# The token loop of an FFT, FFN and MoE kernel: activation by ACT's sine, copies and subtraction on VectorE

## The chip, the core and the metric

The kernel runs on one core of a Trainium2 chip. The metric is the device time of one execution in microseconds (us). A core has five engines, each with an instruction queue of its own that is worked off in order: TensorE (PE in the profile; its weight loads are PEld) multiplies matrices into PSUM; VectorE (DVE) and ScalarE (ACT) work element by element on PSUM and SBUF; GpSimd (POOL) works on SBUF; SyncE (SP) issues DMAs. Engines wait for each other by semaphores.

## What is computed

Eight sequences of 3072 tokens with 256 features go through a filter in the frequency domain, a feed-forward network and a mixture of eight experts with one expert per token.

```python
X = np.fft.rfft(x, axis=1)
y = np.fft.irfft(X * (filt_r + 1j * filt_i), n=3072, axis=1)       # 8 x 3072 x 256
x = y.reshape(24576, 256)
h = x @ w_in                                                       # 256 -> 2048
g = h * np.tanh(np.log1p(np.exp(h)))
x = g @ w_out                                                      # 2048 -> 256
e_idx = np.argmax(x @ w_gate, axis=1)                              # one expert of 8 per token
for e in range(8):
    m = e_idx == e
    ye = np.maximum(x[m] @ w1[e], 0) @ w2[e]
    out[m] = softmax(x[m] @ w_gate)[e] * sigmoid(x[m] @ w_output_gate)[e] * ye
```

The factor tanh(log(1 + e^h)) is (1 - w^2)/(1 + w^2) with w = sigmoid(-h) = (1 - tanh(h/2))/2. Written as an angle it is cos(2 arctan w).

## The kernel before, in words

There are three stages. The opening (to about 150 us) prepares the weights and runs the first sequence's transform (`forward(0)`, `back(0, 0)`). The token loop (to about 2725 us) does the feed-forward network. The expert stage (to the end) runs the experts on tokens that were sorted into `bucket`.

The token loop works on tiles of 256 tokens: 12 tiles per sequence (`NT`), 96 in all. A tile has 8 units (`FP`), each with 256 of the 2048 hidden features, so there are 768 units. One step of the loop handles several units at different depths. `mm1(i)` (L821) makes `h` of unit i, 128x512 in PSUM, by 12 matmuls of fp16 high and low halves; `ps_h` has three banks for it. Then ACT takes `tanh` (L834), `arctan` (L837), `square` (L840) and `factor_c` (L844), and VectorE multiplies `h` by the three factors of a polynomial in `factor_1` (L849), `factor_2` (L853) and `product` (L857), which all read the bank. ACT writes the fp16 high half `gh` (`high_half`, L861), GpSimd the low half `gl` (`low_half`, L865). `mm2(i)` (L878) multiplies both with `w_out` by 12 matmuls into two accumulators per tile, of which there is one set. `LA` = 5: in step p, `mm1` runs for unit p + 5 and `mm2` for unit p. After the last unit of a tile, `evacuate` (L888) has ACT copy both accumulators out.

Beside this runs other work, spread over the steps by generators. `forward(b + 1)` transforms the next sequence: `psa` (L273), a round trip through DRAM (`xs`, `bin`), `psb` (L305), products on VectorE with GpSimd's sum (L311 to L325), `psbi` (L338), `zo` and a second round trip (`zs`, `zin`). `back(b, c)` brings 384 tokens back (`psai` L384, `y_h` on ACT, `y_l` on VectorE) into a ring `y_h`, `y_l`. `weights()` finds scales and writes the experts' weights as fp16 halves (L646, L678, L682). `route(g)` picks the expert of two tiles' tokens by some 20 small VectorE operations, prepares `rows` on GpSimd and ACT, and scatters them into `bucket` by indirect DMAs (L801). `units(p)` starts and advances these generators, `small()` and `big()` give the routing its turns.

The order of the instructions on each engine is written out by hand (`manual_schedule`): it is the order in which the program emits them. `post(engine, work)` puts an operation into a list, and `turn({"A": 1})` emits the next posted one of that kind (A for ACT, V for VectorE, P for GpSimd, T for TensorE, S for SyncE) if it was posted in an earlier step.

Of the kernel before, what the change touches and what calls it, by code (L numbers as in the profile page):

```python
# [22 lines left out]
D = 256  # L23
# [14 lines left out]

KAPPA = 0.2774708104398191 ** 0.5
ROOT1, ROOT2, MID, OFF = 0.17115794576, 1.30006388906, 1.33968847258, 2.69928854473  # L40
# [22 lines left out]
def fft_ffn_moe_kernel(ctx: ExitStack, tc: tile.TileContext, x, fri, w_in, w_out, w_gate, w_ogate, w1, w2,  # L63
# [196 lines left out]
    def forward(b):  # L260
# [37 lines left out]
        for g in range(NG + LAG):  # L298
            if g + 1 < NG:
                bi[g + 1] = load_bin(b, g + 1)  # L300
            if g < NG:
# [6 lines left out]
                def first(ps=ps, f=f, g=g):  # L308
                    need(g - 3)
                    yt[g] = [s1.tile([128, 2 * D], F32, tag=n, name=n, bufs=k) for n, k in (("t1", LAG + 1), ("t2", 3))]  # L310
                    nc.vector.tensor_tensor(out=yt[g][0], in0=ps, in1=f[:, 0].rearrange("p s d -> p (s d)"), op=ALU.mult)  # L311
# [295 lines left out]
    gp = ph.enter_context(tc.tile_pool(name="gp", bufs=4))  # L607
# [104 lines left out]
    def route(g, xq):  # L712
# [19 lines left out]
        r16 = rows.bitcast(F16)  # L732
        yield True
        V.tensor_reduce(out=amax, in_=xq[:, :, 0:D], axis=AX.X, op=ALU.max, apply_absolute_value=True)
        yield
        V.tensor_reduce(out=mx, in_=lg, axis=AX.X, op=ALU.max)
        yield
        V.tensor_scalar(out=amax, in0=amax, scalar1=1e-30, scalar2=None, op0=ALU.max)
        yield
        V.tensor_tensor(out=d, in0=lg, in1=col(mx), op=ALU.subtract)  # L740
# [3 lines left out]
        yield  # L744
        V.scalar_tensor_tensor(out=v, in0=d, scalar=0.0, in1=row("w8"), op0=ALU.is_equal, op1=ALU.mult)

        post("A", lambda: nc.scalar.activation(out=d, in_=d, func=AF.Tanh, scale=gates[:, 0:1]), "exp", delay=1)
# [9 lines left out]
        for s in range(RS):  # L757
# [3 lines left out]
        V.tensor_reduce(out=m2, in_=v, axis=AX.X, op=ALU.max)  # L761
        yield
        post("P", lambda: nc.gpsimd.tensor_copy(rows[:, :, D + 1:D + 2], ids_sb[:, g * RS:(g + 1) * RS].unsqueeze(2)),
             "id")
        V.tensor_tensor(out=oh[:, 0:RS, :], in0=v, in1=col(m2), op=ALU.is_equal)
        count(rank, oh)
        yield
        V.tensor_tensor(out=v, in0=oh[:, 0:RS, :], in1=lo_, op=ALU.mult)
        yield
        V.tensor_reduce(out=sel, in_=v, axis=AX.X, op=ALU.add)  # L770
        post("A", lambda: nc.scalar.activation(out=sel, in_=sel, func=AF.Sigmoid, scale=gates[:, 1:2]), "sig", delay=1)
# [17 lines left out]
        yield from until("r")  # L789
# [5 lines left out]
        yield  # L795
        V.tensor_tensor(out=rank, in0=rank, in1=oh[:, 0:RS, :], op=ALU.mult)
        yield
        with nc.allow_low_precision("whole numbers below 2^24"):
            V.tensor_reduce(out=slot, in_=rank, axis=AX.X, op=ALU.add)
# [6 lines left out]
    LA = 5  # L806
# [3 lines left out]
    h_ps, m_u, m_v, g_h, g_hl, accs = {}, {}, {}, {}, {}, {}  # L810
# [17 lines left out]
    def pair(name, bufs, dt=F32):  # L828
        return mp.tile([128, 2 * T], dt, tag=name, name=name, bufs=bufs)

    def tanh(i):
        m_u[i] = pair("u", 3)
        b = i // (FP * NT)
        nc.scalar.activation(out=m_u[i], in_=wide(h_ps[i]), func=AF.Tanh, scale=seq[b % 2][:, 1:2])  # L834

    def arctan(i):
        nc.scalar.activation(out=m_u[i], in_=m_u[i], func=AF.Arctan, scale=-0.5, bias=0.5)  # L837

    def square(i):
        nc.scalar.activation(out=m_u[i], in_=m_u[i], func=AF.Square, scale=KAPPA)  # L840

    def factor_c(i):
        m_v[i] = pair("v", 4)
        nc.scalar.activation(out=m_v[i], in_=m_u[i], func=AF.Square, bias=-MID)  # L844

    def factor_1(i):

        t = wide(h_ps[i])
        nc.vector.scalar_tensor_tensor(out=t, in0=m_u[i], scalar=-ROOT1, in1=t, op0=ALU.add, op1=ALU.mult)  # L849

    def factor_2(i):
        t = wide(h_ps[i])
        nc.vector.scalar_tensor_tensor(out=t, in0=m_u.pop(i), scalar=-ROOT2, in1=t, op0=ALU.add, op1=ALU.mult)  # L853

    def product(i):
        v = m_v[i]
        nc.vector.scalar_tensor_tensor(out=v, in0=v, scalar=OFF, in1=wide(h_ps.pop(i)), op0=ALU.add, op1=ALU.mult)  # L857

    def high_half(i):
        g_h[i] = gp.tile([128, 2 * T], F16, tag="gh", name="gh")  # L860
        nc.scalar.activation(out=g_h[i], in_=m_v[i], func=AF.Copy)  # L861

    def low_half(i):
        gl = gp.tile([128, 2 * T], F16, tag="gl", name="gl")
        nc.gpsimd.tensor_tensor(out=gl, in0=m_v.pop(i), in1=g_h[i], op=ALU.subtract)  # L865
        g_hl[i] = (g_h.pop(i), gl)

    def mm2(i):
        g, j = divmod(i, FP)
        if j == 0:  # L870
            accs[g] = [ps_acc.tile([128, NA], F32, tag=f"a{s}", name=f"a{s}") for s in range(TS)]
        gh, gl = g_hl.pop(i)
# [29 lines left out]
    gens = {"f": None, "b": back(0, 1), "r": None, "big": False}  # L902
    WE = 10
    WU, UB, BL = 390, 85, 3
# [10 lines left out]
    def units(p):  # L915
# [8 lines left out]
        if t == NT - 2:  # L924
            if j == 5 and b + 1 < NB:
                gens["b"] = back(b + 1, 0)
        elif t == NT - 1:
            if j == 3 and b + 1 < NB:
                gens["b"] = back(b + 1, 1)
        elif t % 3 and j == 1:  # L930
            gens["b"] = back(b, 2 * (t // 3) + 1 + t % 3)
# [21 lines left out]
    for p in range(-LA, nunits):  # L953

        a, c, d, e, l = p + 5, p + 4, p + 3, p + 2, p + 1
        has = [0 <= x < nunits for x in (a, c, d, e, l)]
        if has[0]:
            mm1(a)
        if p >= 1 and p % FP == 0:
            finish(p // FP - 1)  # L960
        if has[2]:
            factor_c(d)
        if has[1]:
            arctan(c)
        if has[2]:
            factor_1(d)
        if has[4]:
            low_half(l)
        if p >= 0:
            small()  # L970
            turn({"A": 1})
        if has[1]:
            square(c)
        if has[2]:
            factor_2(d)
        if p >= 0:
            small()
        if has[3]:
            high_half(e)
        if has[2]:  # L980
            product(d)
        if p >= 0:
            units(p)
            mm2(p)
            big()
            turn({"A": 1})
        else:
            piece()
        if has[0]:
            tanh(a)  # L990
        if p >= 0:
            big()
            tick()
# [298 lines left out]
```

## Time and profile before

| | us |
|---|---|
| median of 3 runs (3836.88 to 3839.9) | 3837.57 |
| the profiled execution | 3847.65 |
| its span, first to last instruction | 3845.9 |

| stage of the profiled execution | TensorE busy | ACT busy | VectorE busy | GpSimd busy |
|---|---|---|---|---|
| 200 to 2700 us, the token loop | 2417.9 | 2340.9 | 2209.2 | 1467.7 |
| 2850 to 2900 us, the expert stage | 50.0 of 50 | 16.4 | 19.5 | 8.7 |

A row of the profile names the line (L821), the engine, the operation, what it writes and reads (out<-in), shapes and types, and a count. Matmuls are pipelined: the time shown for one reaches to its modelled end, while the next has long started. The granted clock is the share of TensorE's full clock that the chip allowed in a stretch. Register, semaphore and DMA-issuing instructions are not counted as busy.

### The profile page before, as it was taken

The page shows a single profiled execution, that of the slowest core. Times are in us where ns is not written, and L with a number is a line of the kernel's source. Part 1 is how long each engine was busy: PE and PEld are TensorE (multiplying, and loading weights), DVE is VectorE, ACT ScalarE, POOL GpSimd, SP SyncE. Part 2 cuts the span into 40 slices and gives each one's busy share as a digit, 9 for nine tenths or more (in the row PEclk, how much of TensorE's full clock was granted, in tenths as well). Part 3 has the DMA queues.
Part 4 walks back from the last instruction along what each step waited for, and adds up shares of the span by engine and source line. Part 5 has one row for each costly group of instructions (what it writes and reads, how often), then busy time and mean ns, then how long its engine had stood idle before and what let it go on. Part 6 is the DMA issues. An engine that isn't in the chain of part 4 may idle for free. (4 is left out here: it accounts for less than half of the span.)

```text
span 3845.9 us, 82929 instructions
## 1 busy us (share of the span) xinstructions
PE 3652.1 (95%) x30764; PEld 3088.9 (80%) x30764; DVE 2786.5 (72%) x5395; ACT 2795.6 (73%) x5443; POOL 1757.1 (46%) x1810
## 2 busy tenths in 40 slices
PE   5699999999999999999999999999799999999998
PEld 3578887887887888787788787877588888888887
DVE  6689888988988988998898898888433333333333
ACT  3489998998998999999899999999433333333332
POOL 2346655655655665565565565555311111111111
PEclk6799999999999999999999999999899999999999
DMA  7434134223313413432432442111333434443341
GB/s 229 128 102 129 51 92 127 74 82 106 112 53 111 127 57 90 140 93 82 128 123 64 120 139 69 52 48 61 86 98 73 116 72 97 116 119 86 84 116 40
DMA packets 300743, 374.32 MB, mean 97 GB/s; under 512 B 158576, under 2 KB 242928, under 8 KB 296624
## 3 DMA queue, kind: packets, MB, share of 16 engines
q1 hardware_dynamic: 281232, 316.62, 30.3%
q0 software_dynamic: 19104, 52.39, 4.0%
q8 instruction: 241, 3.95, 0.5%
q14 instruction: 166, 1.36, 0.1%
HBM read 388.09 MB, written 121.59 MB: 133 GB/s over the span
## 5 line engine op out<-in xcount | busy, mean ns | idle before, releaser
L865 POOL TENSOR_TENSOR gl<-v,gh 128x512 f16<-128x512 f32 x768 | 891.2, 1164 | 658.0 <-ACT gh L861 617.5
L1104 DVE SCALAR_TENSOR_TENSOR hl<-eh,hh 128x256 f16<-128x256 f32 x824 | 350.0, 425 | 667.9 <-ACT hh L1103 664.1
L1103 ACT ACTIVATE hh<-eh 128x256 f16<-128x256 f32 x824 | 315.9, 383 | 667.3 <-PE eh L1094 657.9
L878 PE MATMUL a<-wout_h,gh 128*128 128x272 f16 x3072 | 751.7, 280 | 4.2 <-ACT xq L888 3.3
L878 PE MATMUL a<-wout_l,gh 128*128 128x272 f16 x3072 | 751.0, 279 | 0.0
L878 PEld LDWEIGHTS <-gh 128*128 128x128 f16 x6144 | 602.2, 98 | 178.9 <-issue 48.4
L821 PEld LDWEIGHTS <-win_h 128*128 128x128 f16 x6144 | 585.4, 98 | 182.6 <-DVE v L857 101.5
L821 PE MATMUL h<-y_h,win_h 128*128 128x256 f16 x3072 | 590.0, 274 | 65.2 <-DVE v L857 62.8
L857 DVE SCALAR_TENSOR_TENSOR v<-v,h 128x512 f32<-128x512 f32 x768 | 526.7, 686 | 168.6 <-ACT v L844 140.1
L1138 POOL DMA_INDIRECT out_dram<-ot,meta x206 | 199.7, 969 | 893.3 <-ACT hh L1103 458.0
L834 ACT ACTIVATE u<-h,seq 128x512 f32<-128x512 f32 x768 | 518.8, 676 | 111.1 <-PE h L821 110.0
L821 PE MATMUL h<-y_h,win_l 128*128 128x256 f16 x3072 | 588.1, 273 | 0.0
L821 PE MATMUL h<-y_l,win_h 128*128 128x256 f16 x3072 | 588.1, 273 | 0.0
L849 DVE SCALAR_TENSOR_TENSOR h<-u,h 128x512 f32<-128x512 f32 x768 | 527.6, 687 | 76.1 <-ACT u L840 72.2
L853 DVE SCALAR_TENSOR_TENSOR h<-u,h 128x512 f32<-128x512 f32 x768 | 531.5, 692 | 12.2
L840 ACT ACTIVATE u<-u 128x512 f32<-128x512 f32 x768 | 482.2, 628 | 16.1
L878 PE MATMUL a<-wout_h,gl 128*128 128x272 f16 x3072 | 482.9, 280 | 0.9 <-POOL gl L865 0.8
L844 ACT ACTIVATE v<-u 128x512 f32<-128x512 f32 x768 | 477.7, 622 | 0.0
L837 ACT ACTIVATE u<-u 128x512 f32<-128x512 f32 x768 | 477.0, 621 | 0.0
L861 ACT ACTIVATE gh<-v 128x512 f16<-128x512 f32 x768 | 473.4, 616 | 2.6 <-DVE v L857 2.6
L1094 PE MATMUL eh<-xt,wbuf 128*128 128x256 f16 x3264 | 445.2, 273 | 1.6 <-DMA wbuf<-ws 1.6
L1121 PE MATMUL ya<-wbuf,hh 128*128 128x256 f16 x2176 | 385.8, 273 | 0.0
(174 smaller groups left out, 5517.4 us busy)
## 6 DMA issues: line engine op xcount, KB each, us to landing
wbuf<-ws SPq DMA_DIRECT2D x68, 2048.0 KB
both<-ws SPq DMA_DIRECT2D x36, 2048.0 KB
fri<-in_fri_dram SPq DMA_DIRECT2D x96, 512.0 KB
ew<-in_w_dram SPq DMA_DIRECT2D x128, 256.0 KB
xin<-in_x_dram SPq DMA_DIRECT2D x128, 192.0 KB
xs<-ao SPq DMA_DIRECT2D x128, 192.0 KB
bin<-xs SPq DMA_DIRECT2D x96, 256.0 KB
zs<-zo SPq DMA_DIRECT2D x96, 256.0 KB
```

Source lines behind the costliest of these rows:

```text
L821: nc.tensor.matmul(h_ps[i][:, q, :], lhsT=w[:, k, f * 128:(f + 1) * 128], rhs=y[:, k, r], start=(n == 0), stop=(n == 5))
L834: nc.scalar.activation(out=m_u[i], in_=wide(h_ps[i]), func=AF.Tanh, scale=seq[b % 2][:, 1:2])
L837: nc.scalar.activation(out=m_u[i], in_=m_u[i], func=AF.Arctan, scale=-0.5, bias=0.5)
L840: nc.scalar.activation(out=m_u[i], in_=m_u[i], func=AF.Square, scale=KAPPA)
L844: nc.scalar.activation(out=m_v[i], in_=m_u[i], func=AF.Square, bias=-MID)
L849: nc.vector.scalar_tensor_tensor(out=t, in0=m_u[i], scalar=-ROOT1, in1=t, op0=ALU.add, op1=ALU.mult)
L853: nc.vector.scalar_tensor_tensor(out=t, in0=m_u.pop(i), scalar=-ROOT2, in1=t, op0=ALU.add, op1=ALU.mult)
L857: nc.vector.scalar_tensor_tensor(out=v, in0=v, scalar=OFF, in1=wide(h_ps.pop(i)), op0=ALU.add, op1=ALU.mult)
L861: nc.scalar.activation(out=g_h[i], in_=m_v[i], func=AF.Copy)
L865: nc.gpsimd.tensor_tensor(out=gl, in0=m_v.pop(i), in1=g_h[i], op=ALU.subtract)
L878: nc.tensor.matmul(accs[g][s], lhsT=a[:, q * T + s * 128:q * T + (s + 1) * 128], rhs=w[:, f, :], start=(f == 0 and a is gh and w is wout_h ...
L1094: nc.tensor.matmul(ps, lhsT=w[:, 0, wh * 2 * DE + k * DE + f * 128:wh * 2 * DE + k * DE + (f + 1) * 128], rhs=xt[:, xh * 2 + k, :], start= ...
```

## The change

The activation's factor is no longer a polynomial by VectorE but the cosine itself: ACT takes `tanh`, `arctan` and then a sine of pi/2 - 2u. Arctan and sine are in a table set of ACT other than the one that tanh and sigmoid use, so the set is switched twice per tile, at places that `plan` fixes. VectorE copies `h` out of PSUM as soon as it is there (`copy`), which frees the bank; ACT and VectorE then work on two units at once (128x1024) in SBUF. The product is one VectorE operation, and the low half's subtraction moves from GpSimd to VectorE. The lag between `mm1` and `mm2` grows from 5 to 16 steps. Routing's own tanh and sigmoid get a kind "X" that is emitted only while the first set is active, its maximum over the features (`amax`) moves behind the choice of the expert, and `slot` ahead of the coefficients. `back` starts at other steps, `forward` is spread over 88 instead of 85 steps, `t2` has two buffers instead of three.

```diff
-LA = 5
+LA = 16
-def factor_c(i), factor_1(i), factor_2(i), square(i)
+def copy(i):
+    if i % 2 == 0:
+        hs[i // 2] = pair("hs", 7)
+    nc.vector.tensor_copy(hs[i // 2][:, i % 2, :], wide(h_ps.pop(i)))
+def tanh(k):
+    b = 2 * k // (FP * NT)
+    m_u[k] = pair("u", 5)
+    nc.scalar.activation(out=flat(m_u[k]), in_=flat(hs[k]), func=AF.Tanh, scale=seq[b % 2][:, 1:2])
+def arctan(k):
+    nc.scalar.activation(out=flat(m_u[k]), in_=flat(m_u[k]), func=AF.Arctan, scale=-0.5, bias=0.5)
+def sine(k):
+    nc.scalar.activation(out=flat(m_u[k]), in_=flat(m_u[k]), func=AF.Sin, scale=-2.0, bias=float(np.pi / 2))
 def product(k):
+    m_v[k] = pair("v", 1)
+    nc.vector.tensor_tensor(out=flat(m_v[k]), in0=flat(m_u.pop(k)), in1=flat(hs.pop(k)), op=ALU.mult)
 def high_half(k):
+    nc.scalar.activation(out=flat(g_h[k]), in_=flat(m_v[k]), func=AF.Copy)
 def low_half(k):
-    nc.gpsimd.tensor_tensor(out=gl, in0=m_v.pop(i), in1=g_h[i], op=ALU.subtract)
+    nc.vector.tensor_tensor(out=flat(gl), in0=flat(m_v.pop(k)), in1=flat(g_h[k]), op=ALU.subtract)
...
-gens = {"f": None, "b": back(0, 1), "r": None, "big": False}
-WU, UB, BL = 390, 85, 3
+gens = {"f": None, "b": None, "r": None, "big": False}
+WU, UB, BL = 390, 88, 3
+        if t == 0 and j == 0:
+            gens["b"] = back(b, 1)
...
+plan = [[(tanh, 0), (tanh, 1)], [(tanh, 2)], [(tanh, 3), "trig_and_small"], [(arctan, 0)], [(arctan, 1), (sine, 0)],
+        [(arctan, 2), (sine, 1)], [(arctan, 3), (sine, 2)], [(sine, 3), "sigmoid_and_others"]]
+for s in range(nunits + LA):
+    p, j, g = s - LA, s % FP, s // FP - 1
+    todo = list(plan[j]) if 0 <= g < NG_ else []
+    def act():          # emits the next of todo for pair 4 * g + ..., a name as nc.scalar.preload_act_table_set
...
+    if exists(s):
+        mm1(s)
+    if p >= 1 and p % FP == 0:
+        finish(p // FP - 1)
+    if s % 2 == 0 and exists(s - 14):
+        high_half((s - 14) // 2)
+    if s % 2 and exists(s - 15):
+        low_half((s - 15) // 2)
+    act()
+    if s % 2 and exists(s - 13):
+        product((s - 13) // 2)
+    small()
+    if j < 3:
+        turn({"X": 1})
+    turn({"A": 1})
+    if exists(s):
+        units(s)
+    if p >= 0:
+        mm2(p)
+    small()
+    if exists(s):
+        copy(s)
+    act()
+    big()
+    if j < 2:
+        turn({"X": 1})
+    turn({"A": 1})
+    big()
+    tick()
...
-                    need(g - 3)
-                    yt[g] = [... for n, k in (("t1", LAG + 1), ("t2", 3))]
+                    need(g - 2)
+                    yt[g] = [... for n, k in (("t1", LAG + 1), ("t2", 2))]
```

## Rows read from the trace of the kernel before

**Rows 1.** Page, part 1: busy us (share of the span) and instructions per engine.

```profile
PE 3652.1 (95%) x30764; PEld 3088.9 (80%) x30764; DVE 2786.5 (72%) x5395; ACT 2795.6 (73%) x5443; POOL 1757.1 (46%) x1810
```

**Rows 2.** Table of stretches: stretch, busy per engine; clock, DMA; the sum over 200:2700.

```profile
2500.00:2600.00 100.00, 94.91 (x823) 78.37 (x821) 83.78 (x152) 99.29 (x187) 55.99 (x57) 1.00 0.17 51
...
sum 2500.00, PE 2417.92 PEld 2013.54 DVE 2209.19 ACT 2340.88 POOL 1467.68; mean PE 302.24 PEld 251.69 DVE 276.15 ACT 292.61 POOL 183.46
```

**Rows 3.** Waits of TensorE, 200:2700: us in total, times, longest.

```profile
PE h L821 <- DVE v L857: 62.2, 86, 2.5
PE psb L305 <- DMA bin<-xs: 13.0, 7, 2.9
PE a L878 <- ACT xq L888: 3.3, 7, 0.9
```

**Rows 4.** Waits of VectorE and ACT, 200:2700, the longest of each.

```profile
DVE v L857 <- ACT v L844: 127.8, 208, 2.4
...
ACT u L834 <- PE h L821: 95.4, 136, 5.2
```

**Rows 5.** Line 888: ns min/median/max, first and last start in us.

```profile
L888 ACT ACTIVATE xq<-a,seq x192: 472/485/506, 201.8 to 2725.4; 128x272 f32<-128x272 f32 x192
```

**Rows 6.** Timeline of TensorE, one step: start us, us, what.

```profile
1508.02 0.38 PE L821 MATMUL h<-y_h,win_h 128*128 128x256 f16 x2
...
1509.33 0.28 PE L878 MATMUL a<-wout_h,gh 128*128 128x272 f16 x1
...
1510.72 0.27 PE L821 MATMUL h<-y_h,win_h 128*128 128x256 f16 x1
```

**Rows 7.** Timeline of ACT, two starts in a full queue.

```profile
1499.66 0.62 ACT L837 ACTIVATE u<-u 128x512 f32<-128x512 f32 x1
1500.18 0.57 ACT L390 ACTIVATE y_h<-psai,seq 128x384 f16<-128x384 f32 x1
```

**Rows 8.** Timeline of ACT, a 1024-wide operation and its successor.

```profile
2702.45 1.05 ACT L755 ACTIVATE rows<-xq 128x1024 f16<-128x1024 f32 x1
2703.40 0.62 ACT L840 ACTIVATE u<-u 128x512 f32<-128x512 f32 x1
```

**Rows 9.** Timeline of ACT, start of the program: the only table load.

```profile
0.74 1.28 ACT L112 ACT_TABLE_LOAD   x1 [0.74 <-PEq L1279]
```

**Rows 10.** Groups by line and shape: count | busy us, mean ns | idle before.

```profile
L865 POOL TENSOR_TENSOR gl<-v,gh 128x512 f16<-128x512 f32 x768 | 891.2, 1164 | 658.0 <-ACT gh L861 617.5 <-issue 18.0 <-PE a L878 14.1
...
L849 DVE SCALAR_TENSOR_TENSOR h<-u,h 128x512 f32<-128x512 f32 x768 | 527.6, 687 | 76.1 <-ACT u L840 72.2 <-issue 2.0
...
L284 DVE COPY ao<-psa 96x512 f32<-96x512 f32 x112 | 76.1, 680 | 0.0
...
L436 DVE SCALAR_TENSOR_TENSOR df<-ds,df 128x1024 f32<-128x1024 f32 x8 | 9.8, 1219 | 0.4
...
L499 ACT ACTIVATE win_h<-w,scale 128x1024 f16<-128x1024 f32 x4 | 4.4, 1140 | 5.2 <-DVE scale L468 5.2
```

**Rows 11.** Line 682, and its longest run on the timeline beside GpSimd.

```profile
L682 DVE SCALAR_TENSOR_TENSOR ew<-ew,wscale,ew x64: 739/747/1680, 1462.7 to 2685.8; 128x512 f16<-128x512 f32 x64
...
1645.77 1.15 POOL L865 TENSOR_TENSOR gl<-v,gh 128x512 f16<-128x512 f32 x1
1645.79 1.68 DVE L682 SCALAR_TENSOR_TENSOR ew<-ew,wscale,ew 128x512 f16<-128x512 f32 x1
```

**Rows 12.** Timeline, start of the token loop: DMA issues of SyncE, then TensorE.

```profile
162.21 0.98 SPq L257 DMA_DIRECT2D zin<-zs  x2
163.94 2.67 SPq L243 DMA_DIRECT2D xin<-in_x_dram  x4
...
168.07 1.99 PE L384 MATMUL psai<-cai,zin 96*128 96x96 f32 x8 [9.65 <-DMA zin<-zs]
```

**Rows 13.** Timeline of TensorE: first mm2 after the last mm1.

```profile
2714.26 0.28 PE L878 MATMUL a<-wout_h,gh 128*128 128x272 f16 x1
```

**Rows 14.** Table of stretches: after a pause of 2.92 us that ended at 596.00.

```profile
596.00:601.00 5.00, 5.00 (x25) 3.53 (x26) 3.36 (x5) 0.32 (x1) 1.33 (x2) 0.66 0.78 273
```

More of the change, by code (lines that the diff above doesn't have):

```diff
@@ L732, in route @@
         r16 = rows.bitcast(F16)
+        yield
+        V.tensor_reduce(out=mx, in_=lg, axis=AX.X, op=ALU.max)
+        yield
+        V.tensor_tensor(out=d, in0=lg, in1=col(mx), op=ALU.subtract)
+        yield
+        V.scalar_tensor_tensor(out=v, in0=d, scalar=0.0, in1=row("w8"), op0=ALU.is_equal, op1=ALU.mult)
+        post("X", lambda: nc.scalar.activation(out=d, in_=d, func=AF.Tanh, scale=gates[:, 0:1]), "exp")
+        yield
+        V.tensor_reduce(out=m2, in_=v, axis=AX.X, op=ALU.max)
+        yield
+        post("P", lambda: nc.gpsimd.tensor_copy(rows[:, :, D + 1:D + 2], ids_sb[:, g * RS:(g + 1) * RS].unsqueeze(2)),
+             "id")
+        V.tensor_tensor(out=oh[:, 0:RS, :], in0=v, in1=col(m2), op=ALU.is_equal)
+        count(rank, oh)
+        yield
+        V.tensor_tensor(out=v, in0=oh[:, 0:RS, :], in1=lo_, op=ALU.mult)
+        yield
+        V.tensor_reduce(out=sel, in_=v, axis=AX.X, op=ALU.add)
+        post("X", lambda: nc.scalar.activation(out=sel, in_=sel, func=AF.Sigmoid, scale=gates[:, 1:2]), "sig")
         yield True
@@ L760, in route @@
         yield
-        V.tensor_reduce(out=m2, in_=v, axis=AX.X, op=ALU.max)
+        yield from until("r")
+        V.tensor_tensor(out=rank, in0=rank, in1=oh[:, 0:RS, :], op=ALU.mult)
         yield
[L763 to L771, printed above, removed]
+        with nc.allow_low_precision("whole numbers below 2^24"):
+            V.tensor_reduce(out=slot, in_=rank, axis=AX.X, op=ALU.add)
         yield
@@ L788, in route @@
         yield
-        yield from until("r")
         yield from until("id")
@@ L794, in route @@
                                in1=inv.unsqueeze(2), op0=ALU.mult, op1=ALU.mult)
[L795 to L799, printed above, removed]
         for s in range(RS):
@@ L826, in wide @@
         return t.rearrange("p q t -> p (q t)")
[L828 to L864, printed above, removed]
-        nc.gpsimd.tensor_tensor(out=gl, in0=m_v.pop(i), in1=g_h[i], op=ALU.subtract)
-        g_hl[i] = (g_h.pop(i), gl)
+    def pair(name, bufs):
+        return mp.tile([128, 2, 2 * T], F32, tag=name, name=name, bufs=bufs)
+    def flat(t):
+        return t.rearrange("p u t -> p (u t)")
@@ L951, in big, with exists @@
             gens["big"] = next(gens["r"], False)
[L953 to L958, printed above, removed]
+    plan = [[(tanh, 0), (tanh, 1)], [(tanh, 2)], [(tanh, 3), "trig_and_small"], [(arctan, 0)], [(arctan, 1), (sine, 0)],
[4 more added lines that the diff above has]
+        def act():
+            if todo:
+                o = todo.pop(0)
+                if isinstance(o, str):
+                    nc.scalar.preload_act_table_set(o)
+                else:
+                    o[0](4 * g + o[1])
+        def exists(x):
+            return 0 <= x < nunits
+        if exists(s):
+            mm1(s)
         if p >= 1 and p % FP == 0:
             finish(p // FP - 1)
[L961 to L968, printed above, removed]
-        if p >= 0:
[L970 to L983, printed above, removed]
-            mm2(p)
[L985 to L993, printed above, removed]
+        if s % 2 == 0 and exists(s - 14):
[11 more added lines that the diff above has]
+            units(s)
+        if p >= 0:
+            mm2(p)
+        small()
[8 more added lines that the diff above has]
+        tick()
     finish(NG_ - 1)
```

33 lines of the change are left out of this document (13 added, 20 removed).

## The prediction

> **What bounds the kernel now.** I began with the page's busy shares: TensorE 95%, ACT 73% and VectorE 72% over the whole span [rows 1]. That average mixes three stages, so the table of stretches came next. Between 200 and 2700 us, the token loop that the change rewrites, TensorE is busy for 2417.92 us of 2500, ACT for 2340.88 (94%), VectorE for 2209.19 (88%); in the last batch, which has no forward transform beside it, ACT is at 99% and TensorE at 95% [rows 2]. So two engines are nearly full, and the reader should ask which one waits for the other. The table of waits says: both, in turn. TensorE's largest wait is mm1 (line 821) waiting for `product` (L857), 62.2 us in 86 pauses, because one of only three `h` banks is held until that product has read it; the others are the transform's input (13.0 us) and the evacuation (3.3 us) [rows 3]. In return ACT's `tanh` waits 95.4 us for mm1, and VectorE's `product` 127.8 us for ACT [rows 4]. It is a loop: bank, four ACT operations and three VectorE operations, bank.
>
> How much can go? Idle TensorE by the table is 2500 - 2417.92 = 82 us. A matmul is shown as lasting 0.27 us, while in a full stream the next starts 0.11 us after it, so every pause hides about 0.16 us more: some 100 pauses [rows 3], 16 us. That makes 98 us, and pauses under 0.16 us are not shown at all; I allow 20 for those. All the rest is matmul work that the change leaves alone. The evacuations mark the tiles: 96 tiles, from 201.8 to 2725.4 us, so 95 intervals of 26.56 us [rows 5], or 3.32 us for each of a tile's 8 steps. A step whose matmuls stream shows the floor: mm1 takes from 1508.02 to 1509.33 and mm2 until 1510.72, 2.70 us [rows 6]; the rest is the transforms between. With (82 + 16 + 20)/95 = 1.2 us of pauses taken off, a tile needs 25.4 us of TensorE. The gain is bounded by about 118 us, 3% of the kernel, whatever ACT and VectorE save.
>
> **ACT.** Per step five 128x512 operations go; their starts are 0.52 us apart [rows 7], so 2.6 us. What comes is four operations per two steps on 128x1024. The nearest row of that size starts its successor 0.95 us later [rows 8]; `tanh` reads its scale from a tile, and the row of such a copy (1140 ns less the same 0.10 of overlap) makes it 1.04 [rows 10]. The trace has no sine. `tanh`, `arctan`, `square` and `copy` all have the same price, so I take the sine at that price too; below it is excluded by the same rows, and above it I know only the bound given by the rival below. Sum: (3 x 0.95 + 1.04)/2 = 1.94 us per step. The table switches are two per tile. The one load in the trace lasts 1.28 us [rows 9], with 0.74 us idle ahead of it; 1.28 and 2.02 are the ends, and I take 1.28, because the idle time ahead belongs to the start of the program. That is 0.32 us per step. ACT's busy time per step is now 3.32 x 94% = 3.11 us; it becomes 3.11 - 2.6 + 1.94 + 0.32 = 2.77, or 22.2 us per tile against TensorE's 25.4. At 2.02 it is 23.7. ACT drops out as the bound.
>
> At this place the rows and the Trainium skill differ. The rows know a load of 1.28 us and no cost around it. The Trainium skill (ScalarE: Activation LUTs, "What ACT_TABLE_LOAD costs") states the same 1283 ns and adds a drain of 1380, 2.66 us for every switch, and its rule is to batch calls by set rather than to switch; no run here shows the drain. By that page ACT would need about 24.9 us per tile, still under 25.4 but with hardly any room; that is the second case below.
>
> **VectorE and GpSimd.** Three operations of 0.69 us with one operand in PSUM go (2.06 us per step), and GpSimd's `gl` (1164 ns, 768 times) goes from its queue [rows 10]. What comes on VectorE: a copy out of PSUM, nearest row L284 with 680 ns; and for each pair of steps a product and a subtraction on 128x1024 with both operands in SBUF, nearest row L436 with 1219 ns [rows 10]. Sum 0.68 + 1.22 = 1.90 per step, 0.16 less than now, so VectorE's need falls from 3.32 x 88% = 2.93 to about 2.8 of 3.17 us. There is one cost more. A VectorE operation with two SBUF operands can stand still until GpSimd's instruction has ended: L682 took 1.68 us beside a `gl` and a scaling, against a median of 0.747 [rows 11]. Both new operations are of this kind. But GpSimd loses its largest work: of 1467.68 busy us in the loop [rows 2] `gl` takes up to 891.2 [rows 10], so some 577 stay, 23% of the time. A wait of about half a GpSimd operation (0.5 us) in 23% of the 768 operations is 0.1 us per step. The small routing operations, which now meet `gl` often, get cheaper by about as much. I count zero for this.
>
> **Where the stall goes.** mm1 of step s+3 now waits only for the copy of step s, and the copy stands on VectorE behind at most one subtraction and one product (odd steps). Behind the product's wait for the sine are queued that copy and, two steps later, mm1. The sine is issued a step ahead; with ACT at 22.2 of 25.4 us its first sine of a tile ends about a step before VectorE wants it. So the 62.2 + 86 x 0.16 = 76 us go, and 5 of the unseen ones: -81. I charge 10 for new short waits: the evacuation now stands on ACT behind a table load, and ACT does 3.9 us of work in the first step of a tile; the ends are 0 and 30. The 13 us of `bin` waits stay, since the distance between the store and the load is 88/49 steps instead of 85/49. Late after that comes TensorE itself.
>
> **Fill and drain.** The lag grows from 5 to 16 steps. Fill: now TensorE does four mm1 and then stands 9.65 us, until 168.07, for `zin`, issued at 162.21, with `xin` behind it at 163.94 [rows 12]. In the new order forward(1) comes ahead of back(0, 1) in step 0, so its psa, waiting for `xin`, stands on TensorE's queue after the first mm1, and `xin` is issued ahead of `zin` on SP's: about as long a wait with three mm1 less done, +3 us (0 to 6). From there TensorE has sixteen mm1, and ACT's first tile fits beside them. Drain: now six mm2 remain after the last mm1, from 2714.26 [rows 13] to the last evacuation at 2725 [rows 5], 8.3 us of work in some 10.5. Afterwards sixteen remain, 22.2 us of work, while ACT still has a whole tile of about 19 us to do and the last accumulators wait for an evacuation queued behind it: eight mm2 (11.1 us) start about 21 us in, so about 33 us, 11 more than the work. TensorE pauses twice there, and after a pause of 2.9 us the granted clock was 0.66 in the next five us (part of it at the lower of its two levels) [rows 14]: 2 to 4 us more. Less today's 2, I take +13 (8 to 18). Routing order and one `t2` buffer less: the reduction of 1.2 us moves behind the small ones, which delays the final scatter by about 1 us, and the opening stage may wait for GpSimd once or twice: +3 together, and 0 to 6.
>
> **The sum.** -81 + 10 + 3 + 13 + 3 = -52; with 3 us for the slow-clock spells that the vanished long pauses caused, -55. The profiled execution took 3847.65 us around a span of 3845.9, 10 us above the median of 3837.57; I carry the difference over to the median: 3837.6 - 55 = 3783.
>
> **The rivals.** (a) The forecast: TensorE is the bound and keeps 30 to 60 us of pauses, 3755 to 3800. Chance 0.60. (b) ACT stays close: a switch keeps ACT longer than the load row shows, 2.7 us, short of the 2.9 at which ACT would pass TensorE. Then ACT needs 22.2 + 2 x 1.4 = 25 us per tile. In the first 84 tiles that barely fits; in the last 12, without a forward transform, TensorE needs only some 23 us (8 x 2.70 = 21.6 and the transform back; an estimate), so up to 12 x 1.5 = 18 us are lost, and 5 in drain and evacuations: 3806. ACT's 99% in the last batch [rows 2] speaks for it, the load row of 1.28 [rows 9] against it. The page named above states this case as its rule. Chance 0.19. (c) No change: the copy takes over the product's role. If product or subtraction meets GpSimd or waits for a late sine once a tile by 0.8 us beyond the two steps of slack, 96 x 0.8 = 77 us come back: about 3838. VectorE at 88% speaks for it, the three banks held only for a copy against. Chance 0.09. (d) Slower: ACT becomes the bound. Without loads it has 19.6 us of work per tile; from 2.9 us per switch it passes TensorE's 25.4, from about 3.4 the loop with its longer drain is slower than today's 26.56. At 4.0 us: 27.6 per tile, 95 x 1.0 + 17, some 3950. The same follows if arctan and sine do not share a set and more loads are put in. Chance 0.12.
>
> A measurement of this kernel can tell about 0.2% (7.7 us) from no change. Faster is (a) and (b), 0.79; same 0.09; slower 0.12. The range reaches from 3752 (-118, 25 us of pauses left, +8 for the drain) to 3815 (case (b) and 9 us more of new waits or drain); (c) and (d), 0.21, are left out.
>
> **What would show it.** Right: ACT's busy share in the loop falls to some 85%, the wait of L821 on VectorE shrinks below 15 us, tiles of 25.4 to 25.8 us. Loads of 1.28 us followed at once by an `arctan` decide (b) and (d). A new wait of L878 on the evacuation, or of the product on the sine, would make (c). The eight last mm2 standing some 10 us after the sixteenth from the end show the drain.

## The result, and the profile after

The changed kernel takes 3797.4 us (median of 4 runs, 3795.03 to 3800.24) against 3838.74 us (4 runs, 3836.88 to 3842.78) for the kernel before on the same chip: a ratio of 0.9891 with a 95% interval of 0.9874 to 0.9908, or 41 us less. The forecast was 3783, faster, in a range of 3752 to 3815. The profiled execution took 3795.03 us around a span of 3793.3; before it was 3847.65 around 3845.9. So the profiles differ by 52.6 us where the sum of the prediction said 55, and the medians by 41.

First the page's busy shares of the changed kernel, which answer [rows 1], and the table of stretches, which answers [rows 2]: stretch, then busy time of TensorE, its weight loads, VectorE, ACT and GpSimd, with granted clock and DMA at the end.

```profile
PE 3630.7 (96%) x30764; PEld 3099.9 (82%) x30764; DVE 2622.3 (69%) x4627; ACT 2455.7 (65%) x3331; POOL 1059.8 (28%) x1042
...
2500.00:2600.00 100.00, 96.48 (x863) 83.47 (x862) 77.63 (x133) 89.98 (x105) 25.43 (x26) 1.00 0.19 59
...
sum 2500.00, PE 2423.80 PEld 2047.54 DVE 2078.13 ACT 2042.46 POOL 807.77; mean PE 1211.90 PEld 1023.77 DVE 1039.06 ACT 1021.23 POOL 403.88
```

ACT falls from 94% to 82% of the loop (2042.46 of 2500), VectorE from 88% to 83%, GpSimd from 59% to 32%. The second line is the last batch, the place where ACT was at 99%. TensorE's sum hardly rises because the loop now ends 56 us earlier, inside the same stretch. That end is seen in the evacuations, which answer [rows 5]:

```profile
L882 ACT ACTIVATE xq<-a,seq x192: 469/482/489, 225.1 to 2669.2; 128x272 f32<-128x272 f32 x192
```

They run from 225.1 to 2669.2 us, 25.73 us per tile (before 26.56). TensorE's waits between 200 and 2660 us answer [rows 3]: engine, tile and line, what it waited for, us in total, times, longest.

```profile
PE psai L381 <- ACT zo L340: 12.6, 7, 2.5
PE a L872 <- ACT xq L882: 11.6, 8, 7.0
PE psai L381 <- DMA zin<-zs: 9.9, 13, 1.6
PE psb L302 <- DMA bin<-xs: 7.7, 7, 1.5
PE a L872 <- DVE gl L859: 3.0, 4, 1.3
```

The 62.2 us of mm1 (now L818) on VectorE are gone from the list. In their place stand waits that the kernel before did not have: the back transform `psai` for the copy `zo` and for the load `zin`. And these are the groups of the new work (count, then busy us and mean ns, then idle time ahead of it):

```profile
L841 ACT ACTIVATE u<-hs,seq 128x1024 f32<-128x1024 f32 x384 | 423.1, 1139 | 3.5 <-DVE hs L836 3.5
...
L844 ACT ACTIVATE u<-u 128x1024 f32<-128x1024 f32 x384 | 401.2, 1045 | 1.0
L847 ACT ACTIVATE u<-u 128x1024 f32<-128x1024 f32 x384 | 391.1, 1042 | 0.0
L956 ACT ACT_TABLE_LOAD x192 | 246.3, 1283 | 3.4
...
L836 DVE COPY hs<-h 128x512 f32<-128x512 f32 x768 | 522.1, 682 | 150.6 <-PE h L818 145.4
L851 DVE TENSOR_TENSOR v<-u,hs 128x1024 f32<-128x1024 f32 x384 | 494.6, 1288 | 25.7 <-ACT u L847 6.9
L859 DVE TENSOR_TENSOR gl<-v,gh 128x1024 f16<-128x1024 f32 x384 | 472.3, 1230 | 13.3 <-ACT gh L855 12.0
```

The sine (L847) costs 1042 ns beside 1045 for the arctan, the load 1283 ns, the copy 682: each is the row that the prediction took as nearest.

By stage, from the profiles: up to the first mm1 2.3 us less; from there to the last evacuation 53.9 less; from the last evacuation to the first expert matmul 3.0 more; the experts 0.6 more. The whole difference is in the token loop.

### The profile page after: what moved, and what is told of

Its sections match the earlier page's. It is cut to its first block, busy times and chain, and to the rows that moved or that the text cites. A ratio compares the mean times of both kernels' runs of the same rounds, so it can differ in the third digit from the quotient of the medians.

```text
span 3793.3 us, 77349 instructions
## 1 busy us (share of the span) xinstructions
PE 3630.7 (96%) x30764; PEld 3099.9 (82%) x30764; DVE 2622.3 (69%) x4627; ACT 2455.7 (65%) x3331; POOL 1059.8 (28%) x1042
## 5 line engine op out<-in xcount | busy, mean ns | idle before, releaser
L872 PE MATMUL a<-wout_h,gh 128*128 128x272 f16 x3072 | 750.7, 280 | 12.6 <-ACT xq L882 11.6
L818 PEld LDWEIGHTS <-win_h 128*128 128x128 f16 x6144 | 598.9, 98 | 86.2 <-issue 7.0
L855 ACT ACTIVATE gh<-v 128x1024 f16<-128x1024 f32 x384 | 405.0, 1055 | 364.5 <-PE a L872 153.2
L836 DVE COPY hs<-h 128x512 f32<-128x512 f32 x768 | 522.1, 682 | 150.6 <-PE h L818 145.4
L818 PE MATMUL h<-y_h,win_h 128*128 128x256 f16 x3072 | 587.7, 273 | 1.3 <-DVE y_l L390 1.3
L818 PE MATMUL h<-y_l,win_h 128*128 128x256 f16 x3072 | 587.7, 273 | 0.0
L818 PE MATMUL h<-y_h,win_l 128*128 128x256 f16 x3072 | 587.6, 273 | 0.0
L851 DVE TENSOR_TENSOR v<-u,hs 128x1024 f32<-128x1024 f32 x384 | 494.6, 1288 | 25.7 <-ACT u L847 6.9
L859 DVE TENSOR_TENSOR gl<-v,gh 128x1024 f16<-128x1024 f32 x384 | 472.3, 1230 | 13.3 <-ACT gh L855 12.0
L841 ACT ACTIVATE u<-hs,seq 128x1024 f32<-128x1024 f32 x384 | 423.1, 1139 | 3.5 <-DVE hs L836 3.5
L844 ACT ACTIVATE u<-u 128x1024 f32<-128x1024 f32 x384 | 401.2, 1045 | 1.0
L847 ACT ACTIVATE u<-u 128x1024 f32<-128x1024 f32 x384 | 391.1, 1042 | 0.0
L798 POOL DMA_INDIRECT bucket<-rows,slot x192 | 230.8, 1202 | 523.5 <-DMA bucket<-rows,slot 341.5
L761 POOL TENSOR_SCALAR xq<-xq,sm 128x256 f32<-128x256 f32 x192 | 223.3, 1174 | 495.0 <-DVE sm L758 489.3
```

Of the source, the lines that this page charges most:

```text
L818: nc.tensor.matmul(h_ps[i][:, q, :], lhsT=w[:, k, f * 128:(f + 1) * 128], rhs=y[:, k, r], start=(n == 0), stop=(n == 5))
L836: nc.vector.tensor_copy(hs[i // 2][:, i % 2, :], wide(h_ps.pop(i)))
L841: nc.scalar.activation(out=flat(m_u[k]), in_=flat(hs[k]), func=AF.Tanh, scale=seq[b % 2][:, 1:2])
L844: nc.scalar.activation(out=flat(m_u[k]), in_=flat(m_u[k]), func=AF.Arctan, scale=-0.5, bias=0.5)
L847: nc.scalar.activation(out=flat(m_u[k]), in_=flat(m_u[k]), func=AF.Sin, scale=-2.0, bias=float(np.pi / 2))
L851: nc.vector.tensor_tensor(out=flat(m_v[k]), in0=flat(m_u.pop(k)), in1=flat(hs.pop(k)), op=ALU.mult)
```

## The experiments

The theory (A): mm1 waited for a PSUM bank that the product held; the copy frees it, and ACT, cheaper even with two table loads per tile, is no longer the bound. The rival (B): ACT is still the bound or close to it, and the table switches cost the rest of the gain. Other theories came up on the way and stand in the expectations. The kernel before, measured beside each group of runs, lay between 3838.7 and 3843.6 us, so a difference between times of different groups is uncertain by some 5 us; the ratios allow for that. In the table, ACT's need per tile is its busy share of 200 to 2600 us times the tile length, which is (last evacuation start - first)/95.

| kernel | median us | ratio to before (interval) | us per tile | ACT's need |
|---|---|---|---|---|
| before | 3838.7 to 3843.6 | 1 | 26.56 | 24.8 |
| changed | 3797.4 | 0.9891 (0.9874 to 0.9908) | 25.73 | 21.3 |
| no switches | 3785.4 | 0.9861 (0.9844 to 0.9877) | 25.65 | 18.6 |
| loads doubled | 3860.6 | 1.0044 (1.0031 to 1.0057) | 26.39 | 23.8 |
| loads tripled | 4016.9 | 1.0453 (1.0436 to 1.0471) | 27.93 | 26.3 |

**No switches.** The sine becomes a second arctan of the same size and the loads go, so the kernel computes another function. No load is needed then: the kernel before ran its tanh and all its arctans on the one load of [rows 9], so the first set holds an arctan too, and it is the sine that makes the two switches necessary.

```diff
-        ...activation(out=flat(m_u[k]), in_=flat(m_u[k]), func=AF.Sin, scale=-2.0, bias=float(np.pi / 2))
+        ...activation(out=flat(m_u[k]), in_=flat(m_u[k]), func=AF.Arctan, scale=-2.0, bias=0.5)
...
-                    nc.scalar.preload_act_table_set(o)
+                    pass
```

> The changed kernel without its two table switches per tile: the sine becomes a second arctan, so the activation's factor is another one and the output is not the reference's. ACT's need, from start to start, falls from 21.0 to 18.4 us per tile. Theory A (the gain came from freeing the h bank early, TensorE is now the bound and ACT has room): 0 to 10 us less than the changed kernel (3797), mostly from the drain, the transform back's wait for zo and the evacuations. Rival B (the time follows ACT's need; the change brought it from 24.1 to 21.0 per tile and the time down by 41 us): 34 us less, about 3763.

Measured: 3785.4 us, 12 below the changed kernel, where A had 0 to 10 and B 34. All 192 loads together are worth 12 us, though ACT is 246 us less busy. With 18.6 us of need in a tile of 25.65, ACT hardly decides any more; that speaks for A in the changed kernel itself.

**Loads twice and three times, by repeating the instruction.**

```diff
                     nc.scalar.preload_act_table_set(o)
+                    nc.scalar.preload_act_table_set(o)
```

> The changed kernel with each table load issued twice, four loads per tile: ACT's need 21.0 + 2.6 = 23.6 us per tile against TensorE's 25.3 (some 22.5 in the last batch). Theory A: 5 to 15 us more than the changed kernel, in the last batch, the drain and the short waits, about 3807. Rival B: 34 more, about 3831. If a load costs 2.66 us and not 1.29, ACT needs 26.3 and A too gives 60 or more.

> Each table load issued three times, six per tile: ACT's need 26.2 us per tile, just over TensorE's 25.3 with the forward transform and well over the 22.5 of the last batch. Theory A: ACT becomes the bound; 12 x 3.7 = 44 us in the last batch and up to 84 x 0.9 = 76 before it, so 60 to 120 more, 3857 to 3917: the step from two loads to three costs far more than the step from one to two. Rival B: 68 more than the changed kernel in even steps, about 3865.

Neither added a load: the traces still hold 192 in the loop, so a repeated load of the set already in place does not appear there. What ran was the changed kernel again, at 3798.19 and 3794.6 us: three measurements of the same work (3797.4 with the first) lie within 3.6 us.

**Loads doubled and tripled, with other sets in between** (the doubled one has the first of the two added lines alone).

```diff
+                    nc.scalar.preload_act_table_set("exp_and_others")
+                    nc.scalar.preload_act_table_set("gelu_and_others")
                     nc.scalar.preload_act_table_set(o)
```

> The changed kernel with a load of a third table set ahead of each of the two, so four real loads per tile (in the two runs that only named a set twice the second load was dropped, and they stand as repeats of the changed kernel). ACT's need from start to start is 21.0 + 2 x 1.29 = 23.6 us per tile, against TensorE's 25.3 (some 22.5 in the last batch). Theory A (TensorE is the bound, ACT has room): 5 to 20 us more than the changed kernel's 3797. Rival B (the time follows ACT's need, 41 us for 3.1 us per tile): 34 more, and half of that gained where the loads are left out, where only 12 were gained.

> Two more sets ahead of each of the two, six loads per tile: ACT's need 26.2 us per tile, over TensorE's 25.3 with the forward transform and well over the 22.5 of the last batch. Theory A: ACT becomes the bound, 44 us in the last batch and up to 76 before it, 60 to 120 more than the changed kernel; the prediction's rival (d) put the point where the loop gets slower than before at 3.4 us per switch, and here a switch takes 3.9: at or above 3839. Rival B: 68 more, about 3865, in the same even step as from two loads to four.

Now the loads are there. From the groups of the doubled kernel:

```profile
L956 ACT ACT_TABLE_LOAD x192 | 246.3, 1283 | 3.5
L957 ACT ACT_TABLE_LOAD x192 | 246.3, 1283 | 1.0
```

The first 246 us of loads cost 12 us, the second 63 (3860.6 - 3797.4; 59 by the ratios), the third 156. Both theories missed: A had 5 to 20 us for the second and 60 to 120 for both, B 34 and 68. The kernel with a need of 23.8 us on ACT is slower than the one before, though mm1's wait for the bank is absent from its list of waits too, VectorE's and GpSimd's work is that of the changed kernel, and TensorE by the prediction needs 25.4. Where the loss lies is seen in the last start of the forward transform's last matmul (`psbi`) and of mm1, first in the changed kernel, then in the doubled one (ns min/median/max, first and last start):

```profile
L335 PE MATMUL psbi<-t,both x384: 379/379/796, 63.9 to 2283.5; 128*128 128x256 f32 x192
...
L818 PE MATMUL h<-y_h,win_h x3072: 269/273/421, 150.2 to 2633.3; 128*128 128x256 f16 x192
```

```profile
L335 PE MATMUL psbi<-t,both x384: 378/379/795, 64.3 to 2319.5; 128*128 128x256 f32 x192
...
L818 PE MATMUL h<-y_h,win_h x3072: 269/273/422, 150.5 to 2694.8; 128*128 128x256 f16 x192
```

Up to the end of the forward transforms the doubled kernel loses 2319.5 - 2283.5 = 36.0 us, in some 83 of the 96 tiles; from there to the last mm1 it takes 375.3 us instead of 349.8, so it loses 25.5 in the other 13. So ACT bites some four times as hard per tile (1.9 us against 0.4) where TensorE has no forward transform to do, as rival (b) had it, but it bites in the full tiles too, where rival (b) had it barely fit. TensorE's largest wait between 200 and 2600 us names one place:

```profile
PE a L872 <- ACT xq L882: 31.8, 23, 3.0
```

The evacuation, queued on ACT behind the loads, makes mm2 wait: the trace has the two loads close ahead of it in all 23 cases. So it is not only how much ACT has to do. The added loads come in lumps, and one lump stands right ahead of the evacuation; whether the same work at other places would cost as much was not tried.

TensorE's clock takes a part too. From 200 us to the last mm1 TensorE idles for 79.0 us in the doubled kernel and for 40.2 in the changed one, and the granted clock stands at its lower level (1.2 GHz) for 44.4 us instead of 6.8. At that level the matmuls of mm2 start 0.23 us apart, against 0.12 at the higher one (2656.48 and 2656.71 in the rows on the drain below; 1509.33 to 1509.45 in the kernel before), so this is some 18 us of the loss, an estimate. These are the two kernels between 200 and 2600 us, the changed one first; the clock is the third figure from the end:

```profile
200.00:2600.00 2400.00, 2359.82 (x19846) 1995.59 (x19845) 2017.34 (x3291) 1982.59 (x2256) 769.44 (x754) 1.00 0.32 96
200.00:2600.00 2400.00, 2325.49 (x19374) 1956.63 (x19373) 1973.57 (x3218) 2162.24 (x2380) 760.64 (x741) 0.99 0.32 94
```

**Only the bank.** The kernel before, with four `h` banks instead of three (one fewer for the transforms), and no other edit of its work.

```diff
+    most = [2]
...
-        while len(live) >= 2:
+        while len(live) >= most[0]:
...
-    ps_h = ph.enter_context(tc.tile_pool(name="ps_h", bufs=3, space=PSUM))
-    open_banks(3, ph, "ps_f")
+    ps_h = ph.enter_context(tc.tile_pool(name="ps_h", bufs=4, space=PSUM))
+    open_banks(2, ph, "ps_f")
+    most[0] = 1
```

> The kernel before with one thing changed: four PSUM banks for h instead of three, taken from the transforms, which keep two and hold one at a time. ACT's, VectorE's and GpSimd's work stay as they were. Theory A (the h bank was what TensorE waited for): the 76 us of mm1's waits fall to some 25, all but the last batch, where ACT is full; the time falls by 30 to 50 us to 3790 to 3810, about as far as with the whole change, less what the transforms lose with one bank. Rival B (ACT's need was the bound): ACT has the same need, so within 10 us of 3839.

Measured: 3847.29 us, ratio 1.0012 (1.0003 to 1.0022): nothing gained, as rival B had it. TensorE's waits between 200 and 2600 us:

```profile
PE psai L385 <- DVE y_l L394: 26.5, 15, 3.3
PE a L880 <- ACT xq L890: 16.5, 21, 1.7
...
PE h L823 <- DVE v L859: 3.5, 7, 1.1
```

The wait of [rows 3] falls from 62.2 us (55.9 of them up to 2600) to 3.5, and the time stays. TensorE's idle time in 200 to 2600 us is 70 us, before it was 76. But the run does not free the bank alone. The 26.5 us for `y_l`, of which the list of the kernel before has nothing, come most likely from the bank taken from the transforms; the 16.5 us for the evacuation (before 2.4) are ACT's, whose need here is the old one. The granted clock, too, stands at its lower level for 37.5 us from 200 us to the last mm1, before for 13.7, which by the rows above costs some 11 us. So a fourth bank at this price gains nothing, and a part of the wait moves to ACT. What a bank would bring that costs the transforms nothing is not shown.

**The subtraction on GpSimd,** as it was before, all else as changed.

```diff
-        nc.vector.tensor_tensor(out=flat(gl), in0=flat(m_v.pop(k)), in1=flat(g_h[k]), op=ALU.subtract)
+        nc.gpsimd.tensor_tensor(out=flat(gl), in0=flat(m_v.pop(k)), in1=flat(g_h[k]), op=ALU.subtract)
```

> One part undone: the low half's subtraction goes back to GpSimd, now 128x1024 for a pair. VectorE's need falls by 0.6 us per step; GpSimd's operation takes about 2.3 us per pair, and the product on VectorE, which starts beside it with two SBUF operands, may stand for it. Theory A: TensorE stays the bound, since the copy has two steps of slack: 0 to 15 us more than the changed kernel. Rival C (VectorE's place in the queue is what counts): the copy behind the standing product becomes late, mm1 waits for it again, 40 or more.

Measured: 3873.18 us, ratio 1.0085 (1.0069 to 1.0102), 76 us over the changed kernel. That looks like a verdict for VectorE. The groups say otherwise:

```profile
L859 POOL TENSOR_TENSOR gl<-v,gh 128x1024 f16<-128x1024 f32 x384 | 818.7, 2132 | 454.2 <-ACT gh L855 402.5 <-issue 50.1
...
L851 DVE TENSOR_TENSOR v<-u,hs 128x1024 f32<-128x1024 f32 x384 | 486.3, 1266 | 498.1 <-POOL gl L859 479.6 <-ACT u L847 17.7
```

The product waits 479.6 us for GpSimd: there is one `v` buffer, and the next product may not write it until GpSimd, with 2132 ns, has read it. So the next run gives `v` a second buffer (the room comes from `bin`).

```diff
-        t = s1.tile([128, 2, D], F32, tag="bin", name="bin", bufs=3)
+        t = s1.tile([128, 2, D], F32, tag="bin", name="bin", bufs=2)
...
-        m_v[k] = pair("v", 1)
+        m_v[k] = pair("v", 2)
...
-        nc.vector.tensor_tensor(out=flat(gl), in0=flat(m_v.pop(k)), in1=flat(g_h[k]), op=ALU.subtract)
+        nc.gpsimd.tensor_tensor(out=flat(gl), in0=flat(m_v.pop(k)), in1=flat(g_h[k]), op=ALU.subtract)
```

> The changed kernel with the subtraction on GpSimd again, as in the run that took 3873, and two buffers for v instead of one (paid for by one bin buffer less), so the next product needn't wait until GpSimd has read v. Theory C1 (the 76 us of that run came from the single v buffer: product waited 442 us for gl): most of it goes, 3800 to 3820, and product's wait for gl falls below 100 us. Rival C2 (the port: product has two SBUF operands and stands still while GpSimd runs, whatever the buffers): the product's own duration stays long and the time stays above 3850.

Measured: 3787.56 us, ratio 0.9856 (0.984 to 0.9873). The 76 us are gone, and the median is 10 us below that of the changed kernel (13 by the ratios; the interval ends where that of the changed kernel, 0.9874 to 0.9908, begins). The same two groups:

```profile
L859 POOL TENSOR_TENSOR gl<-v,gh 128x1024 f16<-128x1024 f32 x384 | 853.0, 2221 | 416.0 <-ACT gh L855 363.7 <-issue 50.3
L851 DVE TENSOR_TENSOR v<-u,hs 128x1024 f32<-128x1024 f32 x384 | 669.4, 1743 | 73.9 <-ACT u L847 54.0 <-POOL gl L859 18.9
```

Both operations got longer side by side (the product 1743 ns instead of 1266), and it costs nothing that shows: VectorE has lost 472.3 us of subtractions, and its busy time in 200 to 2600 us falls from 2017.34 to 1912.97 us all the same. The move of the subtraction to VectorE is no gain by itself; in this kernel it is needed because `v` has a single buffer.

**Three `gh` buffers.** ACT's largest waits in the changed kernel, 200 to 2600 us:

```profile
ACT gh L855 <- PE a L872: 149.4, 103, 3.1
ACT gh L855 <- DVE v L851: 70.8, 42, 4.5
ACT xq L882 <- PE a L872: 53.2, 50, 3.0
```

`gh` has two buffers, so ACT stands until TensorE has read the pair before the last, with tanh, the evacuation and `zo` queued behind it.

```diff
-        g_h[k] = gp.tile([128, 2, 2 * T], F16, tag="gh", name="gh")
+        g_h[k] = gp.tile([128, 2, 2 * T], F16, tag="gh", name="gh", bufs=3)
```

> The changed kernel with three buffers for gh instead of two. Now ACT's high_half of pair k can't start before the second mm2 of pair k - 2 has read its buffer, one step earlier on TensorE; ACT waits 151 us for that. Theory D (this coupling is what makes ACT late for its other work, above all the transforms' zo): ACT's wait for mm2 falls below 40 us, zo's share of psai's wait (12.6 us) and part of the evacuation's (11.6) go, 8 to 15 us less than the changed kernel. Rival E (psai waits because back now falls together with psb, and VectorE is busy): ACT's wait moves to another place, time within 5 us.

Measured: 3783.48 us, ratio 0.9846 (0.9833 to 0.986), the lowest median of all, and an interval clear of the changed kernel's: this version beats both. The waits in the same stretch, TensorE's and then ACT's largest:

```profile
PE psai L381 <- ACT zo L340: 13.0, 7, 2.5
PE psai L381 <- DMA zin<-zs: 5.2, 7, 1.6
PE psb L302 <- DMA bin<-xs: 3.8, 3, 1.5
...
PE a L872 <- ACT xq L882: 1.6, 2, 1.3
```

```profile
ACT gh L855 <- DVE v L851: 168.8, 102, 4.3
```

The 149 us are gone; ACT now waits for its own input, and no wait of TensorE grew by more than 1 us. `zin`, `bin` and the evacuation wait less, `zo` does not. As the expectation's theory D had it, 8 to 15 us were gained (14 by the medians, 17 by the ratios), but not from `zo`. In the doubled-load kernel the same edit gives 15 us: 3845.34, ratio 1.0003 (0.9993 to 1.0012).

```diff
+                    nc.scalar.preload_act_table_set("exp_and_others")
                     nc.scalar.preload_act_table_set(o)
...
+        g_h[k] = gp.tile([128, 2, 2 * T], F16, tag="gh", name="gh", bufs=3)
```

> Four table loads per tile, as in the run that took 3860, and three gh buffers. ACT's need is 23.6 us per tile, under TensorE's 25.3, but with its waits for mm2 the tile took 27. Theory D (ACT's need must be counted with the waits in its queue, and the gh buffers make most of them): 3860 falls by 30 or more, to 3810 to 3830. If it stays above 3850, ACT's own work, unevenly spread over the steps, is enough to hold TensorE.

So the buffers are a quarter of what the second load costs (15 of 63 us), where theory D had expected half or more. Most of it stays with a third buffer, and mm2's wait for the evacuation too (30.2 us after 31.8).

**The back transform later in the tile,** to test whether the waits for `zo` and `zin` can be moved away.

```diff
-        elif t < NT - 2 and t % 3 and j == 6:
-            gens["b"] = back(b, 2 * (t // 3) + 1 + t % 3)
+        elif t > 0 and (t - 1) % 3 and t < NT - 1 and j == 2:
+            gens["b"] = back(b, 2 * ((t - 1) // 3) + 1 + (t - 1) % 3)
```

> The changed kernel with the six inner calls of back per sequence started four steps later (step 2 of the next tile instead of step 6), so that their psai don't fall on steps 41, 64 and 72 of a sequence, where each waits 1 to 2.6 us. Rival E (the coincidence with psb and zo at a tile's start, when ACT has four tanh and a copy queued): the psai waits (23 us for zo and zin) fall below 10, 8 to 15 us less than the changed kernel. Theory D (ACT is late everywhere because of gh): the waits reappear at the new steps, within 5 us.

Measured: 3794.97 us, ratio 0.9867 (0.9851 to 0.9883), not told apart from the changed kernel. TensorE's waits, 200 to 2600 us:

```profile
PE psai L381 <- issue: 12.0, 6, 2.9
...
PE psai L381 <- DVE t L316: 8.5, 7, 1.9
PE psai L381 <- ACT zo L340: 1.5, 1, 1.5
```

`zo` falls from 12.6 to 1.5 and `zin` from 9.9 to 0.9, but the same matmul now waits for others: moved, not removed.

**Together:** two `v` buffers with GpSimd's subtraction, the later back transform, and the bucket padding moved behind the first loads.

```diff
-    pads()
...
+        if s == 4:
+            pads()
```

> A candidate that may beat the changed kernel: subtraction on GpSimd with two v buffers and two bin buffers (10 to 12 us less, as measured), back started four steps later, and the writing of the pads moved behind step 4, so that xin and zin are no longer queued behind 16 DMAs when the loop starts. Expected: TensorE's 12.9 us wait for xin at the loop's start falls to 4 or less (9 us), psai's waits mostly go (up to 8 more): 3765 to 3780. If the pads' DMAs then delay the transform's loads instead, the 9 us come back within the first sequence.

Measured: 3794.88 us, ratio 0.9872 (0.9857 to 0.9887), no better than without the last two edits, and short of the 3765 to 3780 that were expected. The fill shows its part: the 12.85 us for `xin` became 3.85, but TensorE now waits 21.0 us for the subtraction in the loop, where it waited 11.9.

## Why the prediction was right, and where it was not

**The vanished wait (-81): right in place and size.** Counted from start to start on TensorE's timeline, the pauses between an mm2 and the next mm1 went from 80.8 us to 0.2.

**The prices: right.** Sine as arctan, load 1.28 us, copy 0.68, products 1.23 to 1.29 us. The load on the timeline of ACT (start us, us, what):

```profile
1520.92 0.71 ACT L675 ACTIVATE ew<-ew,wscale 128x512 f16<-128x512 f32 x1
1521.64 1.28 ACT L956 ACT_TABLE_LOAD   x1
1522.94 1.06 ACT L844 ACTIVATE u<-u 128x1024 f32<-128x1024 f32 x1
```

It starts 0.01 us after its predecessor ends, and the arctan starts 1.30 us after it. The Trainium skill (ScalarE: Activation LUTs, "What ACT_TABLE_LOAD costs") adds a drain of 1380 ns; no such gap is here. What a switch costs more than its row is the overlap of two ACTIVATEs (0.1 us by [rows 7, 8]): some 1.4 us. ACT's need was forecast as 22.2 us per tile and is 21.3, VectorE's as 2.8 us per step and is 2.7 (83% of 25.73/8).

**New short waits (+10): undersized.** The waits for `zo` and `zin`, which before did not have, are 22.5 us; the evacuation outside the drain adds 1.3 to [rows 3] (11.6 - 7.0 - 3.3), `gl` 3.0, and `bin` gives 5.3 back: 21.5 net. The prediction charged ACT's crowded first step of a tile to the evacuation; it is the back transform that pays. ACT and TensorE at step 41 of a sequence:

```profile
1543.05 2.17 ACT L841 ACTIVATE u<-hs,seq 128x1024 f32<-128x1024 f32 x2
1545.13 1.04 ACT L764 ACTIVATE rows<-xq 128x1024 f16<-128x1024 f32 x1
1546.08 0.57 ACT L340 ACTIVATE zo<-psbi 128x512 f32<-128x512 f32 x1
...
1546.70 0.46 PE L381 MATMUL psai<-cai,zin 96*128 96x96 f32 x2 [2.04 <-ACT zo L340]
```

Two tanh and the row copy stand ahead of `zo` on ACT; until `zo` is out, its PSUM bank is not free for `psai`. The prediction also did not read the two `gh` buffers as a wait on ACT (149.4 us); the run with three shows that this was worth some 14 us.

**Fill (+3) right, drain (+13) oversized.** The forecast wait for `xin` is there at 12.85 us, 3.2 more than the 9.65 for `zin` before. In the drain the last accumulators do wait for an evacuation behind a load:

```profile
2654.47 1.28 ACT L956 ACT_TABLE_LOAD   x1
2655.77 0.86 ACT L882 ACTIVATE xq<-a,seq 128x272 f32<-128x272 f32 x2
2656.31 0.39 PE L872 MATMUL a<-wout_h,gh 128*128 128x272 f16 x1 [7.03 <-ACT xq L882]
2656.48 0.43 PE L872 MATMUL a<-wout_l,gh 128*128 128x272 f16 x1
2656.71 0.43 PE L872 MATMUL a<-wout_h,gh 128*128 128x272 f16 x1
```

Counted from start to start, TensorE loses 11.2 us there, before some 2.5: +8.7. The 3 us for the slow clock in the loop were right: from 200 us to the last mm1 the clock stands at its lower level for 13.7 us before and for 6.8 now, worth some 3.4 us. Opening and tail, forecast at +3, came to -2.3 + 3.0 + 0.6 = +1.3. With these sizes the sum would be -55 + 11.5 - 4.3 - 1.7 = -49.5; measured are -52.6, and I cannot assign the last 3 us. That the sum came out within 2.4 us is in part luck: its terms were wrong by +11.5, -4.3 and -1.7 us, which partly cancel, and 3 us remain unassigned.

**The carry to the median failed.** The time is 14.4 us over the forecast, and 2.4 of them are the sum. The other 12: the prediction took the profiled execution of before, 10.1 us above its median, and subtracted that again, as if the changed kernel's profiled execution stood as high. It stood 2.4 us below its median. The medians of before, measured beside the kernels of this study, lie between 3838.7 and 3843.6, so its profiled 3847.65 was a high one; why, stays open.

**"ACT drops out as the bound": true for this kernel, for a reason too simple.** The sum compared ACT's work with TensorE's, and let ACT fill up to 25.4 us per tile; rival (b) at 25 us was priced at 3806 (3812 by its own figures, since 25 is 2 us and not 1.5 above the 23 that it gives TensorE), and rival (d) was to decide at 3.4 us per switch. With two loads, 2.57 us per switch and a need of 23.8, the kernel is already at 3860. The step that failed is "barely fits": with the work placed as it is, ACT's room ends before 23.8 us, well short of TensorE's 25.4. The changed kernel, at 21.3, is 12 us above the one without loads; from 21.3 to 23.8 some 63 of 246 further us of loads show in the time, from 23.8 to 26.3 it is 156 of 246. Why the room ends there is shown only in part: ACT's queue is in order and stands in each tile for mm2 and for VectorE (the list of ACT's waits above), the third `gh` buffer takes a quarter of the loss away, the evacuation behind the loads is 31.8 us of TensorE's waits, and the slower clock some 18 us.

The reason given for the gain is also only a part of the cause. The new order, with mm1's wait for the bank gone and VectorE's and GpSimd's work as in the changed kernel, brought nothing once ACT's need was put back near the old one by loads: so the gain needs ACT's saving, unless it is the place of the added loads that undid it. Whether it needs the free bank as well is argued, not shown: the run with a fourth bank also took one from the transforms, and the saving alone in the old order was not tried.

## What to carry to other kernels

When one engine waits for a buffer that another frees late, ask first whether the freeing engine is full: another buffer may then only move the wait, as the fourth bank did in part. Before adding work to an engine in order, look at what stands right behind it in the queue, as the evacuation stood behind the loads. Such an engine must keep room beside its work; count where its queue stands for others, and count the buffers behind each of its outputs, before calling it off the path. When an operation moves between engines, see how many buffers its input has: a single one made GpSimd look 76 us worse than it is.

## What the chip showed that was not expected

A second load of the table set already in place does not appear in the trace (192 loads in the loop, whether the kernel text asks for 192, 384 or 576; where it is dropped the traces do not say), while loads of different sets in a row each cost their 1283 ns. And it is not VectorE's operations alone that get longer in company: the two on GpSimd below take 1174 and 1202 ns on average in the changed kernel and took 926 and 1018 before, though GpSimd has less to do. What is new beside them are VectorE's operations with two SBUF operands; that these are the cause was not tested by itself.

```profile
L798 POOL DMA_INDIRECT bucket<-rows,slot x192 | 230.8, 1202 | 523.5 <-DMA bucket<-rows,slot 341.5
L761 POOL TENSOR_SCALAR xq<-xq,sm 128x256 f32<-128x256 f32 x192 | 223.3, 1174 | 495.0 <-DVE sm L758 489.3
```
